# Cutting the second layer's 2304 tokens into blocks of 512, 512, 384, 320, 320 and 256 in place of four of 512 and one of 256

## Chip, cores and metric

The kernel runs on one core of one Trainium2 chip. The metric is the device time of one execution in microseconds (us); lower is better. Durations of single instructions are in nanoseconds (ns). Engines: PE is TensorE (matmuls; PEld are its weight loads), DVE is VectorE, ACT is ScalarE, POOL is GpSimd, SP is SyncE, which issues most transfers (DMA).

## What is computed

An attention over q, k, v (4 batches, 8 heads, 576 positions, 64 channels) gives a matrix of 2304 tokens by 512 channels. Two feed-forward layers follow, all in float32:

```python
x = attn_out.transpose(0, 2, 1, 3).reshape(B * S, H * D)   # 2304 x 512
h = x @ moe_w_in            # 512 -> 2048
x = np.maximum(0.01 * h, h) @ moe_w_out    # 2048 -> 512
h = x @ moe2_w_in
out = (h - np.tanh(h)) @ moe2_w_out
```

The change touches only the second layer (the last two lines).

## The kernel before

**Blocks.** Each layer goes over the tokens in blocks (PLAN, L40). The first layer has five blocks, 464 tokens and four times 460 (BLOCKS, L34). The second has four of 512 and one of 256 (BLOCKS2, L39). They run one after the other in the loop at L515. Attention work for a later block is woven into the first layer; it is not part of the second.

**One block.** The 2048 hidden units are 16 steps f of 128. In each step `gemm1` (L413) makes a 128 x n tile `hp` of hidden values, and `gemm2` (L425) adds the contribution of step f - 2 (LAG = 2) to four accumulators `acc`, each 128 x n. Operands are float32r; to keep precision each is split in a high and a low part, and a product is three matmuls: high by high, low weight by high, high weight by low. So `gemm1` has 4 chunks of channels x 3, and `gemm2` 4 output chunks x 3 matmuls for one pass over the n tokens. Every matmul loads its own 128 x 128 weights first.

**Halves.** `parts` decides how many passes: a width that is a multiple of 256 goes in pieces of 256, any other in one piece:

```python
HALF = 256
def parts(n):
    if n % HALF:
        return [slice(0, n)]
    return [slice(o, o + HALF) for o in range(0, n, HALF)]
```

A block of 512 thus takes 24 matmuls of 256 columns for each `gemm1` and each `gemm2`; one of 460 takes 12 of 460 columns; one of 256 takes 12 of 256.

**Between the two products.** In the second layer ACT takes the tanh of `hp` into `tg` (L538), DVE subtracts (`tg` = hp - tanh, L539), ACT rounds it to the high part `gh` (L541) and DVE makes the low part `gl` (L542). `hp` has two buffers, `tg` three.

**From block to block.** The next block's input `xf` comes back from DRAM (`load_x2`, L402) a whole block ahead. In the last step `convert` (L395) splits it into `xh` and `xl` (L392 on ACT, L393 on DVE). When the block's last `gemm2` is done, the four accumulators are copied to `ev` (L564 on ACT; in the very last block two of the four on DVE, L566) and sent to `out` by SP (L570). `ev` shares the three buffers of `tg`: the fourth copy needs the transfer of the first to have landed, and the next block's first two tanh need those of the second and third. The accumulators have one buffer, so the next block's first `gemm2` needs the copies done.

**Places.** `placed` (L375) gives each float32r operand tile a starting place of PLACES[idx] x 16 elements in its buffer: 80 elements in the first layer, 64 in the second. The tiles are sized for the widest block (NMAX = 512), so their strides don't depend on the block.

Of the kernel before, what the change touches and what calls it, by code (L numbers as in the profile page):

```python
# [18 lines left out]
NTOK = B * S  # L19
# [16 lines left out]
    _g = UNITS[_i:_i + BU]  # L36
    BLOCKS.append((_g[0][0] * S + _g[0][1] * QB, sum(x[2] for x in _g)))
NB = len(BLOCKS)
BLOCKS2 = [(t, min(512, NTOK - t)) for t in range(0, NTOK, 512)]  # L39
PLAN = [(0, g, n) for g, n in BLOCKS] + [(1, g, n) for g, n in BLOCKS2]  # L40
NMAX = max(n for _, _, n in PLAN)
PLACES = (5, 5, 5, 5, 5, 4, 4, 4, 4, 4)
HALF = 256
NLD = 2
U_PE = 8
# [26 lines left out]
def tile_attention_moe(  # L72
# [300 lines left out]
            wt[moe, f, half] = (hi, lo)  # L373

    def placed(tag, idx, cols, bufs=1):  # L375
        at = PLACES[idx] * 16
        t = sb.tile([128, cols + 128], F32R, tag=tag, name=tag, bufs=bufs)
        return t[:, at:at + cols]

    def new_split(idx):  # L380
        return tuple(placed(t, idx, NC * NMAX).rearrange("p (c n) -> p c n", c=NC) for t in ("xh", "xl"))
# [133 lines left out]
    for idx, (moe, g0, n) in enumerate(PLAN):  # L515
# [9 lines left out]
        for f in range(NF + LAG):  # L525
# [3 lines left out]
            if f < NF:  # L529
                hp = ps_h.tile([128, 512], F32, tag="h", name="hp")  # L530
                gemm1(moe, f, x, n, hp)
                tg = sb.tile([128, NMAX], F32, tag="tg", name="tg", bufs=3)
                gh, gl = (placed(t, idx, NMAX, 3) for t in ("gh", "gl"))
                gs[f] = (gh, gl)
                if moe == 0:
                    nc.scalar.activation(out=tg[:, :n], in_=hp[:, :n], func=ACTF.Prelu, alpha=0.01)  # L536
                else:
                    nc.scalar.activation(out=tg[:, :n], in_=hp[:, :n], func=ACTF.Tanh)  # L538
                    nc.vector.tensor_tensor(out=tg[:, :n], in0=hp[:, :n], in1=tg[:, :n], op=ALU.subtract)  # L539
                marks[:] = [  # L540
                    nc.scalar.copy(out=gh[:, :n], in_=tg[:, :n]),  # L541
                    nc.vector.tensor_tensor(  # L542
                        out=gl[:, :n], in0=tg[:, :n], in1=gh[:, :n].bitcast(F32), op=ALU.subtract
                    ),
                ]
# [94 lines left out]
```

## Time and profile before

| | us |
|---|---|
| median of 3 runs | 930.8 |
| lowest and highest of them | 928.76, 937.88 |
| the profiled execution | 930.39 |
| its span, first to last instruction | 928.6 |
| PE busy in it | 910.5 |

The profile is of one execution. Its own time lies 1.8 us above its span, and 0.4 us under the median of the runs. A row of the chain of waits gives a start, a length and a group of instructions, where each is the one that the next had to wait for. A matmul's own duration includes its way through the array, so matmuls overlap; the pace is read from the distance between starts.

### The profile page before, as it was taken

The numbers are of one execution on the slowest core, as the hardware profiler recorded it, in microseconds if no ns is written. First come the engines' busy times: TensorE is split into PE (matmuls) and PEld (weight loads), VectorE is DVE, ScalarE is ACT, GpSimd is POOL, SyncE is SP. The second block draws the span as 40 slices with busy tenths as digits, with TensorE's granted clock in tenths as the row PEclk, the third lists the DMA queues.
The fourth block names the chain that finished last, engine by engine and source line by source line (L and its number), as shares of the span: only waits on it lengthen the run. The fifth ranks groups of instructions, "written<-read, shape, count | busy, mean of one in ns | idle before, by whom it ended". The sixth has DMA issues, their size and how long they took to land.

```text
span 928.6 us, 16921 instructions
## 1 busy us (share of the span) xinstructions
PE 910.5 (98%) x7326; PEld 831.8 (90%) x7326; DVE 421.5 (45%) x747; ACT 369.0 (40%) x763; POOL 45.7 (5%) x76
## 2 busy tenths in 40 slices
PE   7989999999999999999999999999999999999997
PEld 6777788888887888888888899999999999999997
DVE  6989894444234513611376777532223223222232
ACT  2767754442244314322465655442223223322322
POOL 1011120013000100000000000000000000000000
PEclk9979999999999999999999999999999999999999
DMA  9996263137020201100466710020002000100100
GB/s 304 393 309 182 57 144 99 35 82 173 2 76 2 91 12 64 47 1 1 142 217 217 258 65 1 2 91 1 1 1 92 1 1 23 47 1 1 47 1 24
DMA packets 26186, 76.78 MB, mean 83 GB/s; under 512 B 3200, under 2 KB 7040, under 8 KB 26112
## 3 DMA queue, kind: packets, MB, share of 16 engines
q1 hardware_dynamic: 19392, 52.50, 15.9%
q0 software_dynamic: 6720, 23.21, 10.0%
q8 instruction: 57, 0.93, 0.4%
q14 instruction: 17, 0.14, 0.0%
HBM read 66.26 MB, written 9.44 MB: 82 GB/s over the span
## 4 chain that ended last, share of the span: by engine, by line
PE 91%; ACT 3%; DVE 3%; DMA 2%; issue 1%; SPq 0%; ACTq 0%
PE hp L420 42%; PE acc L432 40%; PE px L267 2%; DMA qk<-qk 1%; PE px L308 1%; ACT wm L340 1%; PE px L294 1%; PE px L209 1%; PE warm L495 1%; DVE wm L357 1%; PE px L173 1%; PE px L201 1%; DMA out<-ev 1%; ACT w L371 1%; DVE wm L350 0%
## 5 line engine op out<-in xcount | busy, mean ns | idle before, releaser
L420 PE MATMUL hp<-xh,w 128*128 128x256 f32 (+2 forms) x1792 | 395.8, 315 | 4.1 <-ACT xh L392 2.2
L432 PE MATMUL acc<-gh,w 128*128 128x256 f32 (+2 forms) x1792 | 386.7, 311 | 0.1
L420 PEld LDWEIGHTS hp<-xh,w 128*128 128x128 f32 x1792 | 292.7, 189 | 22.1 <-issue 4.1
L432 PEld LDWEIGHTS acc<-gh,w 128*128 128x128 f32 x1792 | 293.9, 188 | 13.9 <-ACT gh L541 0.3
L420 PE MATMUL hp<-xl,w 128*128 128x256 f32 (+2 forms) x896 | 281.1, 314 | 0.0
L432 PE MATMUL acc<-gl,w 128*128 128x256 f32 (+2 forms) x896 | 278.4, 311 | 0.0
L542 DVE TENSOR_TENSOR gl<-tg,gh 128x460 fp32r<-128x460 f32 (+3 forms) x160 | 101.7, 636 | 181.9 <-ACT gh L541 176.0
L420 PEld LDWEIGHTS hp<-xl,w 128*128 128x128 f32 x896 | 169.1, 189 | 6.8 <-issue 0.4
L432 PEld LDWEIGHTS acc<-gl,w 128*128 128x128 f32 x896 | 168.1, 188 | 6.8 <-DVE gl L542 0.2
L539 DVE TENSOR_TENSOR tg<-hp,tg 128x512 f32<-128x512 f32 (+1 forms) x80 | 51.0, 637 | 193.4 <-ACT tg L538 193.3
L538 ACT ACTIVATE tg<-hp 128x512 f32<-128x512 f32 (+1 forms) x80 | 44.4, 555 | 172.7 <-PE hp L420 169.2
L541 ACT CAST gh<-tg 128x460 fp32r<-128x460 f32 (+3 forms) x160 | 92.4, 577 | 49.6 <-DVE tg L539 47.9
L536 ACT ACTIVATE tg<-hp 128x460 f32<-128x460 f32 (+1 forms) x80 | 44.3, 553 | 142.6 <-PE hp L420 141.3
L372 DVE TENSOR_TENSOR w<-wm,w 128x512 fp32r<-128x512 f32 x64 | 43.0, 688 | 14.8 <-ACT w L371 13.9
L371 ACT CAST w<-wm 128x512 fp32r<-128x512 f32 x64 | 37.9, 617 | 27.8 <-DVE wm L357 22.3
L357 DVE SCALAR_TENSOR_TENSOR wm<-raw,wm 128x512 int32<-128x512 int32 x64 | 43.1, 685 | 0.7
L340 ACT ACTIVATE wm<-raw 128x512 f32<-128x512 f32 x64 | 40.9, 671 | 3.1 <-DMA raw<-wts 2.3
L564 ACT COPY ev<-acc 128x460 f32<-128x460 f32 (+3 forms) x38 | 20.1, 554 | 45.6 <-PE acc L432 32.4
L393 DVE TENSOR_TENSOR xl<-xf,xh 128x460 fp32r<-128x460 f32 (+3 forms) x40 | 24.2, 633 | 27.3 <-ACT xh L392 27.3
L392 ACT CAST xh<-xf 128x460 fp32r<-128x460 f32 (+3 forms) x40 | 21.7, 575 | 28.3 <-PE hp L420 26.8
L495 PE MATMUL warm<-band_sb,id_bf 128*128 128x192 bf16 x190 | 20.7, 265 | 3.8 <-DVE band_sb L490 3.8
L296 ACT COPY lpt<-px 128x512 f32<-128x512 f32 x16 | 9.4, 586 | 33.3 <-PE px L294 33.3
(77 smaller groups left out, 499.3 us busy)
## 6 DMA issues: line engine op xcount, KB each, us to landing
raw<-wts SPq DMA_DIRECT2D x64, 512.0 KB, 5.6
qs<-qkd POOLq DMA_DIRECT2D x12, 576.0 KB, 6.1
q<-qw POOLq DMA_DIRECT2D x16, 256.0 KB, 4.3
k<-kw POOLq DMA_DIRECT2D x16, 256.0 KB, 5.2
v<-vw POOLq DMA_DIRECT2D x16, 256.0 KB, 4.6
xf<-x2d SPq DMA_DIRECT2D x4, 1024.0 KB, 5.4
out<-ev SPq DMA_DIRECT2D x16, 256.0 KB, 3.1
x2d<-ev SPq DMA_DIRECT2D x16, 230.0 KB, 2.1
```

The lines of the kernel that those rows point to most:

```text
L340: nc.scalar.activation(out=m, in_=st[:, :, 1].bitcast(F32), func=ACTF.Abs, scale=W_SCALE)
L357: nc.vector.scalar_tensor_tensor(out=m, in0=st[:, :, 1], scalar=-0x80000000, in1=m, op0=ALU.bitwise_and, op1=ALU.bitwise_or)
L371: nc.scalar.copy(out=hi, in_=m)
L372: nc.vector.tensor_tensor(out=lo, in0=m, in1=hi.bitcast(F32), op=ALU.subtract)
L420: nc.tensor.matmul(out=hp[:, t], lhsT=w[:, cs], rhs=r[:, c, t], start=(c == 0 and i == 0), stop=(c == NC - 1 and i == 2),)
L432: nc.tensor.matmul(out=acc[m][:, t], lhsT=w[:, cs], rhs=r[:, t], start=(f == 0 and i == 0 and k == 0), stop=(f == NF - 1 and i == 2), skip ...
L495: nc.tensor.matmul(out=p[:, :3 * KB], lhsT=id_bf, rhs=band_sb.rearrange("p a w -> p (a w)"), start=True, stop=True)
L536: nc.scalar.activation(out=tg[:, :n], in_=hp[:, :n], func=ACTF.Prelu, alpha=0.01)
L538: nc.scalar.activation(out=tg[:, :n], in_=hp[:, :n], func=ACTF.Tanh)
L539: nc.vector.tensor_tensor(out=tg[:, :n], in0=hp[:, :n], in1=tg[:, :n], op=ALU.subtract)
L541: nc.scalar.copy(out=gh[:, :n], in_=tg[:, :n]),
L542: nc.vector.tensor_tensor(out=gl[:, :n], in0=tg[:, :n], in1=gh[:, :n].bitcast(F32), op=ALU.subtract),
```

## The change

The second layer's blocks become 512, 512, 384, 320, 320 and 256 tokens. 384 and 320 aren't multiples of 256, so `parts` leaves them whole: 12 matmuls of 384 or 320 columns for each `gemm1` and each `gemm2`. PLACES is now looked up by layer in place of by block, with the same values (80 elements in the first layer, 64 in the second).

```diff
-BLOCKS2 = [(t, min(512, NTOK - t)) for t in range(0, NTOK, 512)]
+SIZES2 = (512, 512, 384, 320, 320, 256)
+BLOCKS2 = [(sum(SIZES2[:i]), n) for i, n in enumerate(SIZES2)]
 PLAN = [(0, g, n) for g, n in BLOCKS] + [(1, g, n) for g, n in BLOCKS2]
 NMAX = max(n for _, _, n in PLAN)
-PLACES = (5, 5, 5, 5, 5, 4, 4, 4, 4, 4)
+PLACES = (5, 4)
...
     def placed(tag, idx, cols, bufs=1):
-        at = PLACES[idx] * 16
+        at = PLACES[PLAN[idx][0]] * 16
```

On every engine the order of the instructions is the same up to the second layer's third block; from there they follow the new widths. ACT's queue at the last joint of two blocks, before (a block of 512 ends, that of 256 begins):

```order
L392 CAST xh<-xf 128x256
L538 ACTIVATE tg<-hp 128x512
L392 CAST xh<-xf 128x256 x3
L541 CAST gh<-tg 128x512
L564 COPY ev<-acc_8018 128x512 x2
L564 COPY ev<-acc_8019 128x512 x2
L538 ACTIVATE tg<-hp 128x256 x2
L541 CAST gh<-tg 128x256 x2
L538 ACTIVATE tg<-hp 128x256
```

and after (a block of 320 ends, that of 256 begins; the source has one line more, so each line number is one higher):

```order
L393 CAST xh<-xf 128x256
L539 ACTIVATE tg<-hp 128x320
L393 CAST xh<-xf 128x256 x3
L542 CAST gh<-tg 128x320
L565 COPY ev<-acc_8172 128x320 x2
L565 COPY ev<-acc_8173 128x320 x2
L539 ACTIVATE tg<-hp 128x256 x2
L542 CAST gh<-tg 128x256 x2
L539 ACTIVATE tg<-hp 128x256
```

Nothing moved here: the queue is the same and only the ending block's tiles are narrower. SP's queue through the second layer, before (`xf` is a block's input, `out` a block's output in four transfers):

```order
L405 DMA xf<-x2d 128x4x512
L570 DMA out<-ev 128x512 x4
L405 DMA xf<-x2d 128x4x512
L570 DMA out<-ev 128x512 x4
L405 DMA xf<-x2d 128x4x256
L570 DMA out<-ev 128x512 x8
L570 DMA out<-ev 128x256 x4
```

and after:

```order
L406 DMA xf<-x2d 128x4x384
L571 DMA out<-ev 128x512 x4
L406 DMA xf<-x2d 128x4x320
L571 DMA out<-ev 128x512 x4
L406 DMA xf<-x2d 128x4x320
L571 DMA out<-ev 128x384 x4
L406 DMA xf<-x2d 128x4x256
L571 DMA out<-ev 128x320 x8
L571 DMA out<-ev 128x256 x4
```

One input transfer and four output transfers are added, and those of the later blocks are smaller; each still stands at its block's joint.

## Rows read from the trace of the kernel before

**Rows 1.** The page: busy time, and the granted TensorE clock in 40 slices.

```profile
PE 910.5 (98%) x7326; PEld 831.8 (90%) x7326; DVE 421.5 (45%) x747; ACT 369.0 (40%) x763; POOL 45.7 (5%) x76
...
PEclk9979999999999999999999999999999999999999
```

**Rows 2.** Stretches of PE: us, busy us (instructions), granted clock, DMA share, GB/s.

```profile
450.00:480.00 30.00, 30.00 (x145) 1.00 0.50 166
...
792.00:876.60 84.60, 84.60 (x749) 1.00 0.01 4
884.00:919.00 35.00, 35.00 (x300) 1.00 0.00 1
```

**Rows 3.** Chain of waits: start us, length us, group; blocks of 464, 460 and 512.

```profile
150.11 7.52 PE acc L432 x36
...
249.51 7.52 PE acc L432 x36
...
615.72 8.16 PE hp L420 x72
...
702.75 8.16 PE hp L420 x72
...
789.79 8.16 PE hp L420 x72
```

**Rows 4.** The same chain in the last block, of 256.

```profile
888.39 1.41 PE acc L432 x12
...
918.08 1.41 PE hp L420 x12
```

**Rows 5.** Timeline of PE at the second layer's start: start us, us, group, idle before.

```profile
527.10 0.28 PE L420 MATMUL hp<-xh,w 128*128 128x256 f32 x1
...
532.64 0.28 PE L420 MATMUL hp<-xl,w 128*128 128x256 f32 x1
533.83 0.51 PE L420 MATMUL hp<-xh,w 128*128 128x256 f32 x2 [0.91 <-DVE tg L539]
```

**Rows 6.** Timeline of PE: four float32 transposes, 128 columns each, in a row.

```profile
128.71 0.62 PE L294 MATMUL px<-id_sb,lpr 128*128 128x128 f32 x4
129.08 0.46 PE L420 MATMUL hp<-xh,w 128*128 128x464 f32 x1
```

**Rows 7.** Timeline of ACT and DVE at the joint of two blocks of 512.

```profile
791.25 0.59 ACT L564 COPY ev<-acc 128x512 f32<-128x512 f32 x1 [0.84 <-DMA out<-ev]
792.60 0.60 ACT L538 ACTIVATE tg<-hp 128x512 f32<-128x512 f32 x1 [0.76 <-PE hp L420]
...
793.23 0.69 DVE L539 TENSOR_TENSOR tg<-hp,tg 128x512 f32<-128x512 f32 x1 [7.32 <-ACT tg L538]
```

**Rows 8.** Timeline of all engines at the joint of 512 and 256.

```profile
876.67 0.39 PE L420 MATMUL hp<-xh,w 128*128 128x256 f32 x2
...
878.31 0.59 ACT L564 COPY ev<-acc 128x512 f32<-128x512 f32 x1 [0.85 <-DMA out<-ev]
...
879.59 0.38 ACT L538 ACTIVATE tg<-hp 128x256 f32<-128x256 f32 x1 [0.70 <-PE hp L420]
880.01 0.42 DVE L539 TENSOR_TENSOR tg<-hp,tg 128x256 f32<-128x256 f32 x1 [8.18 <-ACT tg L538]
...
880.49 0.50 PE L420 MATMUL hp<-xh,w 128*128 128x256 f32 x2 [0.93 <-DVE tg L539]
...
881.48 0.38 ACT L538 ACTIVATE tg<-hp 128x256 f32<-128x256 f32 x1 [1.50 <-DMA out<-ev]
...
882.21 0.50 PE L432 MATMUL acc<-gh,w 128*128 128x256 f32 x2
```

**Rows 9.** DMA issues: queue, count, KB each, median us to landing.

```profile
xf<-x2d SPq DMA_DIRECT2D x4, 1024.0 KB, 5.4
out<-ev SPq DMA_DIRECT2D x16, 256.0 KB, 3.1
...
out<-ev SPq DMA_DIRECT2D x4, 128.0 KB, 1.8
```

## The prediction, made before the changed kernel ran

> **What bounds the kernel now.** I read the page first: PE is busy 98% of the span and its clock is granted in full but for a slice near the start [rows 1]. Then the stretches: through the second layer PE has no idle time, at a granted clock of 1.00, the 2.4 GHz level, and with next to no DMA traffic [rows 2]. So a matmul stream sets the end, and what matters is the distance between the starts of two matmuls, the pace. The chain of waits gives it.
>
> - 512 in halves: from one block's 72 matmuls at 615.72 us to the next block's at 702.75, and again to 789.79, is 87.03 us for 768 matmuls [rows 3]: 113.3 ns for 256 columns. At 2.4 GHz 256 columns stream in 106.7 ns, so 6.6 ns come on top; I call that the excess.
> - 460 in one piece: 36 matmuls in 7.52 us [rows 3], 208.9 ns. Columns alone: 191.7. Excess 17.2 ns. The block of 464 has the same 7.52 us for 36.
> - 256, the last block: from 888.39 to 918.08 are 21 groups of 12, 252 matmuls in 29.69 us [rows 4], 117.8 ns. Excess 11.1. At the second layer's start the halves have that slower pace too: from 527.10 to 532.64 are 47 steps in 5.54 us, 117.9 ns; after the pause that ends at 533.83 the layer goes on at 113.3 [rows 5, 3]. So 256 columns have two paces, and one replaces the other at a pause of PE.
>
> That both widths of the first layer take the same time shows that the pace isn't a plain sum of columns and a constant, so 320 and 384, which no row shows, can only be bounded.
>
> **What the change does, part by part.** The same 2304 columns stream through PE in both kernels. Matmuls fall from (4 x 24 + 12) x 32 = 3456 to (2 x 24 + 4 x 12) x 32 = 3072: two blocks of 512, 2 x 768 matmuls of 256 columns, become 384 matmuls of 384 columns and 768 of 320. The price of the two old blocks is 2 x 87.03 = 174.06 us.
>
> *The new widths.* Columns alone: 384 take 160.0 ns, 320 take 133.3 ns, together 384 x 160.0 + 768 x 133.3 = 163.8 us. To that come 1152 times the excess. Bounds:
> - no excess: 163.8 us, 10.2 less than now. It can't be less, as rows 2 already show the higher clock level.
> - the 6.6 ns of the halves: 163.8 + 1152 x 6.6 = 171.4, that is 2.6 less.
> - the 17.2 ns of 460 columns: 183.7, that is 9.6 more.
> I take a straight line between the two measured widths, 6.6 ns at 256 and 17.2 at 460: 320 columns get 9.9 ns, 384 get 13.3. So 143.3 and 173.3 ns, and 384 x 173.3 + 768 x 143.3 = 66.5 + 110.1 = 176.6 us: **+2.5 us**. Why the line: 320 is nearer to 256 and 384 lies between the two, and each end of the line is a long steady row.
>
> *The joints.* Three joints of two 512s cost nothing: the block-to-block distance is the same 87.03 us as 768 matmuls at the steady pace. That of 512 and 256 costs something [rows 8]. The new block's first matmul starts at 876.67; three gemm1 of 12 matmuls at 113.3 are 4.08 us, so its first gemm2 is due at 880.75 and starts at 882.21, 1.46 us late. The cause is the three shared buffers: the fourth copy of the accumulators starts at 878.31, when the first transfer has landed; the first tanh at 879.59, which the row gives to PE, though the gemm1 it needs ended over a microsecond before: it waits for the second transfer, whose buffer it takes; DVE is then through at 880.43 and the third gemm1 can have its `hp` buffer at 880.49. At the joint of two 512s the same steps happen at nearly the same distances (fourth copy 791.25, first tanh 792.60) [rows 7], but the new block's first two gemm1 last 5.4 us and hide them. Now the joints:
> - 512 to 512, and the layer's start, stay as they are.
> - 512 to 384: two gemm1 last 24 x 173 = 4.16 us. The second transfer lands 2.92 us after the first matmul, as in rows 8; tanh and subtraction of 384 columns together lie between the 0.8 us of 256 columns (0.38 and 0.42) [rows 8] and the 1.3 of 512 (0.60 and 0.69) [rows 7], so the buffer comes free 3.7 to 4.2 us after that matmul: hidden.
> - 384 to 320, 320 to 320, 320 to 256: two gemm1 last 3.4, 3.4 and 2.7 us, but the transfers are 192 and 160 KB in place of 256; a transfer of 128 KB lands in 1.8 us where one of 256 takes 3.1 [rows 9]. Each lies between nothing and 1.46. I take 0.1 for each of the first two, near the joint that hides, and 0.6 for the last, where the pieces are shorter on both sides.
> Together 0.8 in place of 1.46: **-0.7 us**; bounds -1.5 (all hidden) and +4.4 (four joints at 1.46).
>
> *At nothing:* ACT and DVE work per column stays and both are under half busy [rows 1]; the step of a 320 block lasts 24 x 143 ns = 3.4 us, while the operations on its tile are each shorter than the 0.60 and 0.69 us of 512 columns [rows 7]. The input loads are issued a block ahead, and the shortest block lasts 45 us against 5.4 to landing [rows 9]. PLACES keeps its values. If that cover were gone it would show as PE idle inside a block, which no row of the second layer has.
>
> *The rest.* The last block keeps its 117.8 ns if PE still pauses at its start; without a pause it could go at 113.3, which is 384 x 4.5 ns = 1.7 us less. I take 0, since I expect a pause.
>
> Sum: +2.5 - 0.7 = +1.8 us on the profiled execution's 930.39: 932.2. That execution lies 0.4 under the median of the runs, so I don't correct further. About 1%, 9.3 us, is what a measurement of this kernel can tell from no change.
>
> **Rivals.**
> 1. *The halves are paced by their weight loads.* Then wider products cost nearly their columns alone. For it: the next matmul starts 0.37 us after the first of four transposes of 128 columns [rows 6], so these stand 93 ns apart, though they stream half as many columns as the halves, at 113.3. Against it: 460 columns have a larger excess, not a smaller one. Price: excess between 0 and 2.5 ns, -10.2 to -7.3, with the joints 919.5 to 922.4; 921 in the middle.
> The Trainium skill ("TensorE: Matmul & The Clock Gate", section "Back-to-back issue gap") gives N / 2.4 + 2.5 ns for a warm stream. By that rule 320 and 384 columns take 135.8 and 162.5 ns and the new blocks 166.7 us, 7.4 less than now. The trace disagrees at both widths that it has: 113.3 against 109.2 by the rule at 256, 208.9 against 194.2 at 460.
> 2. *The excess of the halves is a constant.* 6.6 ns at every width, fewer matmuls pay it less often: -2.6 - 0.7, 927.1. For it: it is the nearest row to 320. Against it: the 17.2.
> 3. *Slower: every undivided product pays the excess of 460 columns.* Place: each of the 1152 new matmuls. For it: all undivided products of the first layer, 464 and 460, pay 15.6 to 17.2 ns, and the undivided 256 of the last block pays 11.1 where halves pay 6.6. Against it: the excess of 256 columns in halves and whole differ by a pause, not by the division. Price +9.6 - 0.7: 939.3; from an excess of 8.4 ns on it is slower than before, and from 17.5 on by over 1%.
> 4. *It doesn't keep the halves' pace.* The two blocks of 512 that stay are 1536 matmuls; if the pause at 533.83 left them at 117.8 they would cost 1536 x 4.5 = 6.9 us more: 939.1. Against it: the code up to the third block is the same, and the trace shows 113.3 there for 340 us.
>
> **How the numbers follow.** The line 0.48, rival 1 0.10, rival 2 0.20, rival 3 0.15, rival 4 0.07. Faster by over 1% only by rival 1 at its far end: 0.04. Slower by over 1%: half of rival 3 and a part of rival 4, where joints come on top: 0.10. Within 1%: 0.86. The range leaves out rival 1 and the far side of rivals 3 and 4: from 926.5 (rival 2 with every joint hidden) to 939.5.
>
> **What would show it.** In the changed profile the chain should have groups of 12 in about 2.08 us in the block of 384 and 1.72 us in those of 320 (1.60 and 2.0 would be columns alone, 1.81 and 2.13 the excess of 460); the two blocks of 512 still 87.0 us each; a pause of PE of under 1 us with DVE `tg` as its releaser at the last joint, and next to none at the others. The forecast is wrong if the pace of 320 columns lies outside 140 to 151 ns, or if PE waits at joints for more than 4 us in all.

## The result and the profile after

| | before | after |
|---|---|---|
| median, us (20 runs each) | 929.73 | 938.85 |
| lowest and highest | 926.08, 947.01 | 933.0, 945.94 |
| profiled execution | 930.39 | 937.83 |
| its span | 928.6 | 936.1 |

The ratio of after to before is 1.0087, 95% interval 1.0061 to 1.0113: slower by 0.9%, about 8 us. The ratio leaves out the two executions of the kernel before that lie over 1.5% above its fastest (944.37 and 947.01 us), and it is one of means, so it isn't the quotient of the two medians. The forecast was 932.2 within 926.5 to 939.5, and no change that can be told; with 20 runs each, 0.9% can be told. The range holds the result, but near its upper end, and both terms of the sum were too low.

The chain of waits of the changed kernel (start us, length us, group), to be read against [rows 3, 4]:

```profile
532.12 4.20 PE hp L421 x24
536.32 3.15 PE acc L433 x24
...
615.63 8.16 PE hp L421 x72
...
702.67 6.24 PE hp L421 x36
...
769.23 5.50 PE hp L421 x36
774.73 1.76 PE acc L433 x12
...
820.49 5.30 PE acc L433 x36
...
825.86 3.53 DMA out<-ev
...
878.29 5.30 PE acc L433 x36
...
883.66 4.20 DMA out<-ev
...
888.85 2.93 PE hp L421 x12
891.78 1.57 PE acc L433 x12
893.35 1.36 PE hp L421 x12
...
927.35 3.41 PE acc L433 x30
```

The two blocks of 512 end at 702.67 us, where they ended before (702.75): the halves keep 113.3 ns, apart from the layer's start. Then every width shows its pace. 384 columns: 36 matmuls in 6.24 us, 173.3 ns, exactly the line's value. 320 columns: 12 in 1.76, 146.7 ns, where the line had 143.3. The block ends stand at 769.23 (384), 825.79 and 883.59 (the two of 320).

The time splits so, all from this chain and the one before:

- pace: 384 x 173.3 + 768 x 146.7 ns = 66.56 + 112.64 = 179.20 us in place of 174.06: **+5.1** (forecast +2.5);
- joints inside the new blocks: they last 883.59 - 702.67 = 180.92, so 1.72 us on top of the pace;
- the last block, to its 378th matmul (the end of the group of 30): 883.59 to 930.76 is 47.17 us; in the chain of before it was 876.83 to 923.03, 46.20. +0.97. With the line above the joints and the last block's pace give **+2.7** (forecast -0.7 and 0);
- the third block starts 0.08 earlier and the program ends 0.23 sooner behind that matmul: -0.3. (The 0.08 is what two larger differences leave, which the change has no part in: the first layer's last groups end 2.6 us earlier in this execution, and the second layer's start loses as much: PE pauses for 1.84 us where before had 0.91 [rows 5], and the groups at 532.12 and 536.32 take 4.20 and 3.15 us where 24 matmuls take 2.72, as the granted clock falls to 0.50 behind that pause.)

Together 7.5 us, the difference of the two spans.

The +2.7 hides two larger amounts. The joints inside the new blocks cost 0.24 us (384 to 320: 825.79 - 769.23 is 56.56, and 384 x 146.7 ns is 56.32) and 1.48 (320 to 320). In the last block, 378 matmuls at 113.3 ns would take 42.84 us. The changed kernel has 4.33 more, all of it from the joint and the clock behind it (below), as the steady groups stand at 1.36; the kernel before had 3.36 more, 1.46 of it from the joint [rows 8] and about 1.9 from the slower pace. So the joints cost 6.05 us in place of 1.46, which is +4.6, and the last block's pace gave back 1.9.

The two joints that cost most, in the timeline of the changed kernel (start us, us, engine line, group; in brackets the idle time before and what ended it):

```profile
827.62 0.43 ACT L565 COPY ev<-acc 128x320 f32<-128x320 f32 x1 [1.38 <-DMA out<-ev]
829.50 0.44 ACT L539 ACTIVATE tg<-hp 128x320 f32<-128x320 f32 x1 [1.45 <-DMA out<-ev]
...
830.51 0.55 PE L421 MATMUL hp<-xh,w 128*128 128x320 f32 x2 [1.23 <-DVE tg L540]
...
887.96 0.78 ACT L539 ACTIVATE tg<-hp 128x256 f32<-128x256 f32 x2 [2.43 <-DMA out<-ev]
...
888.85 0.79 PE L421 MATMUL hp<-xh,w 128*128 128x256 f32 x2 [2.45 <-DVE tg L540]
```

It is the chain of [rows 8]: the tanh waits for the second transfer to leave its buffer, DVE for the tanh, PE for DVE. It is now there at two joints, and PE's pause at the last is 2.45 us in place of 0.93. The chain above has the transfers that the two tanh waited for: 3.53 us from issue to landing at the first of the two joints, 4.20 at the second. In the kernel before the second transfer was issued at 876.67 and the tanh that waited for it started at 879.59 [rows 8], 2.9 us at most. So smaller transfers didn't land sooner. DMA issues of the changed kernel (KB each, median us to landing):

```profile
out<-ev SPq DMA_DIRECT2D x8, 256.0 KB, 2.9
...
out<-ev SPq DMA_DIRECT2D x8, 160.0 KB, 2.8
...
out<-ev SPq DMA_DIRECT2D x4, 128.0 KB, 1.7
```

The median of 160 KB is no lower than that of 256. A median mixes the four transfers of a joint, though. The first one lands at much the same time whatever its size: the fourth copy, which waits for it, starts 2.1 us after its issue at 256 KB (876.18 to 878.31 in the kernel before) and 1.9 at 160 KB (883.23 to 885.11). The second is the one that differs. The cover, two gemm1 of the next block, shrinks with the width; what it has to cover doesn't, and at these two joints it grew.

The DMA packets show what held it. At every joint of the second layer one packet of 16 KB, of the queue that carries instructions, falls among the four transfers. At the two costly joints it ran from 827.17 to 828.19 us and from 884.79 to 886.63, that is from 1.3 and 1.1 us after the issue of the second transfer; at the other joints of the two kernels it came 1.9 to 2.5 us after. At the last joint, 46 of the 48 small closing packets of the first three transfers (4 bytes, 16 for each) were done by 885.65; from then to 886.6 only the instruction packet moved, and the second transfer landed at 887.85.

The runs below have the same contrast. In 12 cases of the 13 traces the packet came within 1.5 us of the second transfer's issue, all behind blocks of 288, 320 or 384: it landed after 3.5 to 4.2 us. Where the packet came later, it landed after 1.9 to 3.2, but for two cases (4.1 in run 3, 4.9 in run 11). Run 6 has such a later packet (1.6 us) at the joint of the two 320s: its second transfer, of 160 KB too, landed after 1.95 us and PE didn't pause there. No run was made to move the packet, so this rests on what differs between the traces.

The long pause has a second price. Stretches around it (us, PE busy and count, granted clock, DMA share, GB/s):

```profile
888.00:889.00 1.00, 0.15 (x1) 0.81 0.02 8
889.00:890.00 1.00, 1.00 (x5) 0.50 0.00 0
...
892.00:893.00 1.00, 1.00 (x10) 0.98 0.00 0
```

After the pause the granted clock is 0.50, the 1.2 GHz level, for over 3 us: the group at 888.85 takes 2.93 us and that at 891.78 takes 1.57, where 1.36 is the steady length. That is 1.8 us on top of the pause itself. The length of the pause alone doesn't decide it: behind pauses of 1.88 and 2.30 us at the same joint in runs 6 and 7 below, the granted clock stays at 1.00, while behind one of 1.76 us in run 3 it falls to 0.50 too. What decides isn't shown.

### The profile page after: what moved, and what is told of

It is laid out like the page before. It is cut to its first block, busy times and chain, and to the rows that moved or that the text cites. A ratio compares the mean times of both kernels' runs of the same rounds, so it can differ in the third digit from the quotient of the medians.

```text
span 936.1 us, 16307 instructions
## 1 busy us (share of the span) xinstructions
PE 915.2 (98%) x6942; PEld 837.0 (89%) x6942; DVE 426.7 (46%) x783; ACT 375.7 (40%) x803; POOL 45.9 (5%) x76
## 4 chain that ended last, share of the span: by engine, by line
PE 87%; DMA 9%; DVE 1%; ACT 1%; issue 1%; POOL 0%; SPq 0%; ACTq 0%; POOLq 0%; DVEq 0%
PE hp L421 41%; PE acc L433 40%; DMA vs<-vd 3%; DMA qs<-qkd 2%; PE px L268 2%; DMA v<-vd 1%; PE px L309 1%; DMA out<-ev 1%; PE px L295 1%; PE px L210 1%; DMA qk<-qk 1%; PE px L174 1%; DMA x2d<-ev 1%; PE px L202 1%; DVE v L150 0%
## 5 line engine op out<-in xcount | busy, mean ns | idle before, releaser
L421 PE MATMUL hp<-xh,w 128*128 128x256 f32 (+4 forms) x1664 | 397.4, 328 | 7.8 <-DVE tg L540 5.5
L433 PE MATMUL acc<-gh,w 128*128 128x256 f32 (+4 forms) x1664 | 387.3, 323 | 0.0
L421 PE MATMUL hp<-xl,w 128*128 128x256 f32 (+4 forms) x832 | 271.5, 327 | 0.0
L433 PE MATMUL acc<-gl,w 128*128 128x256 f32 (+4 forms) x832 | 268.4, 323 | 0.0
L543 DVE TENSOR_TENSOR gl<-tg,gh 128x460 fp32r<-128x460 f32 (+5 forms) x176 | 104.3, 593 | 184.6 <-ACT gh L542 184.0
L540 DVE TENSOR_TENSOR tg<-hp,tg 128x512 f32<-128x512 f32 (+3 forms) x96 | 53.5, 558 | 195.6 <-ACT tg L539 195.6
L542 ACT CAST gh<-tg 128x460 fp32r<-128x460 f32 (+5 forms) x176 | 95.5, 542 | 53.0 <-DVE tg L540 51.2
L539 ACT ACTIVATE tg<-hp 128x512 f32<-128x512 f32 (+3 forms) x96 | 47.1, 491 | 172.6 <-PE hp L421 167.1
L394 DVE TENSOR_TENSOR xl<-xf,xh 128x460 fp32r<-128x460 f32 (+5 forms) x44 | 24.6, 590 | 26.7 <-ACT xh L393 26.7
L393 ACT CAST xh<-xf 128x460 fp32r<-128x460 f32 (+5 forms) x44 | 22.1, 540 | 27.7 <-PE hp L421 26.2
```

What stands on the lines that cost most here:

```text
L394: nc.vector.tensor_tensor(out=xl[:, c, :n], in0=src[:, c, :n], in1=xh[:, c, :n].bitcast(F32), op=ALU.subtract)
L421: nc.tensor.matmul(out=hp[:, t], lhsT=w[:, cs], rhs=r[:, c, t], start=(c == 0 and i == 0), stop=(c == NC - 1 and i == 2),)
L433: nc.tensor.matmul(out=acc[m][:, t], lhsT=w[:, cs], rhs=r[:, t], start=(f == 0 and i == 0 and k == 0), stop=(f == NF - 1 and i == 2), skip ...
L543: nc.vector.tensor_tensor(out=gl[:, :n], in0=tg[:, :n], in1=gh[:, :n].bitcast(F32), op=ALU.subtract),
```

## The experiments

The theory after the trace: A, an undivided product pays 13.3 ns on top of its columns from 288 columns or so on, twice what a half of 256 pays (6.7 ns for each started run of 256 columns), and that is about 5 us; and the joints are the other 3. Rivals: the line of the prediction for other widths, the starting place of the operands, the pace alone, the joints alone.

**1. Changed kernel, accumulator copies in buffers of their own** (two attention tiles that are dead in the second layer).

```diff
-            ev = sb.tile([128, NMAX], F32, tag="tg", name="ev", bufs=3)
+            if moe == 1:
+                ev = sb.tile([128, 512], F32, tag="lpr" if m < 2 else "lpt", name="ev", bufs=2)
+            else:
+                ev = sb.tile([128, NMAX], F32, tag="tg", name="ev", bufs=3)
```

> The changed kernel, but the copies of the second layer's accumulators go to four buffers of their own (two tiles of the attention that are dead by then) in place of the three shared with tg. Theory: of the loss, about 5 us are the pace of the new widths and about 3 us the joints, where a tanh waits for a transfer to leave its buffer; then PE has no pause at the four joints inside the layer, the profiled time falls by 3.5 to 5.5 us against the changed kernel's 937.8, and about 3 to 5 us over the kernel before are left. Rival, the pace alone: the time stays within 1.5 us of the changed kernel. Rival, the joints alone: it falls to the time of before.

Measured: 932.21 us, ratio to before 1.0013 (0.9966 to 1.0060); the profiled execution 934.37. The changed kernel had 1.0087, so the buffers take back 0.7%, some 7 us, with wide intervals. The profiled times differ by 3.5 us, the low end of what was expected, though not for the expected reason alone, as the chain shows. The gain speaks against the pace alone; the joints alone aren't excluded by these times. The chain of its profiled execution settles that, and shows something not expected:

```profile
614.98 8.48 PE hp L421 x72
...
705.43 6.29 PE hp L421 x36
...
772.50 5.28 PE hp L421 x36
...
885.14 4.09 PE hp L421 x36
```

No joint costs anything: the two blocks of 320 last 885.14 - 772.50 = 112.64 us, 768 x 146.7 ns. But from the layer's first pause on the blocks of 512 run at 8.48 / 72 = 117.8 ns, the slower pace that before had only at the layer's start and in its last block [rows 4, 5]; the 48 matmuls ahead of that pause stand 113.3 apart. And the last block is back at that faster pace, with no pause in between. That is rival 4's price, paid here by chance or by cause: runs 9 to 11 ask which.

**2. The same edit in the kernel before.**

> The kernel before with the same four buffers of their own for the copies of the second layer. Theory: its one costly joint (512 to 256) goes, and the last block stays at 113.3 ns a matmul if the slower pace of 117.8 came from the pause: 2.7 us faster (1.5 from the pause, the rest from the pace: 1.0 to 1.7). If the slower pace has nothing to do with the pause: 1.0 to 1.5 us faster. Rival, the joints cost nothing: 0.

Measured: 926.93 us, ratio 0.9943 (0.9898 to 0.9987): faster than before, though the interval all but reaches 1. Its chain has the joint of 512 and 256 without a pause, and the last block at 113.3 ns:

```profile
876.78 4.08 PE hp L420 x36
```

The profiled span is 924.9, 3.7 under before's 928.6. The joint and the slow last block were worth 3.4 of that: 378 matmuls at 113.3 are 42.84 us against the 46.20 of before. The expected 2.7 was a little low for the chain; the ratio alone would say 5 us.

**3. A sweep of widths.**

```diff
-SIZES2 = (512, 512, 384, 320, 320, 256)
+SIZES2 = (512, 448, 416, 352, 288, 288)
```

> The second layer in blocks of 512, 448, 416, 352, 288 and 288, all but the first undivided; read for the pace of each width alone. Theory A, every started run of 256 columns costs one fixed amount (6.7 ns; two runs 13.3): 200.0, 186.7, 160.0 and 133.3 ns. Theory B, the line of the prediction from 6.6 ns at 256 to 17.2 at 460: 203.3, 188.3, 158.3 and 128.3 ns. Theory C, the excess goes with where a width ends against some boundary in memory: no order in it, jumps of several ns between neighbours.

Measured: 938.93 us, one run. The steady groups of the four widths, in its chain:

```profile
613.37 7.28 PE hp L421 x36
...
691.02 6.72 PE hp L421 x36
...
770.08 1.92 PE acc L433 x12
...
832.94 1.60 PE hp L421 x12
```

448 columns take 202.2 ns, 416 take 186.7, 352 take 160.0, 288 take 133.3. The last three are theory A's to the digit and not the line's (188.3, 158.3, 128.3); the first is 2.2 ns above A, as far as 460 columns' two paces lie apart (last section); one execution doesn't tell whether 448 has a faster pace as well. So from 288 to 416 columns the excess is one constant in this execution, 13.3 ns, and at 256 it is half of that: a step, not a line. The line met 384 only because it crosses the constant there.

**4. The kernel before with 512 undivided.**

```diff
-HALF = 256
+HALF = 512
```

> The kernel before with the blocks of 512 undivided: 12 matmuls of 512 columns in place of 24 of 256. Theory A (6.7 ns for each started run of 256): 226.7 ns a matmul, 87.0 us a block, as in halves; whole kernel within 2 us of before. Theory B (the line): 19.9 ns on top, 233.2 ns, 89.6 us a block, about 10 us slower.

Measured: 936.35 us, one run; the chain:

```profile
615.20 8.40 PE hp L420 x36
```

233.3 ns: the line's value, not A's. Theory A falls at 512; the excess is 20.0 there, three times 6.7. So A holds as a table of what was measured (6.7 at 256, 13.3 from 288 to 416, 20.0 at 512) and not as a rule on started runs of 256. The time is 6.8 us above before's median on the same chip, where the line's 2.6 us for each of four blocks make 10. For the halves it says the same as the line: two products of 256 (226.7 ns) beat one of 512.

**5. The wide new blocks without the narrow ones.**

```diff
-SIZES2 = (512, 512, 384, 320, 320, 256)
+SIZES2 = (512, 512, 512, 384, 384)
```

> The second layer in blocks of 512, 512, 512, 384 and 384: one part of the change alone, the wide undivided blocks without the narrow ones. Theory (13.3 ns on top of the columns for each undivided product; joints hide where two gemm1 of the next block outlast the transfers): 384 matmuls at 173.3 ns are 66.6 us a block, two of them 133.1 against 130.6 for 512 and 256 at 113.3; no pause of over 0.5 us at a joint, as two gemm1 last 4.16 us, so the 2.7 us of the old last joint go: profiled time within 1.5 us of before. Rival, any undivided block costs a joint of over 1 us whatever its width: 3 to 5 us slower than before.

Measured: 927.19 us, one run, 1.6 under before's median of the same chip (928.78). The chain and the timeline at the joint of the two 384s:

```profile
786.11 6.24 PE hp L421 x36
...
846.42 5.21 PE acc L433 x30
```

```profile
856.52 0.49 ACT L539 ACTIVATE tg<-hp 128x384 f32<-128x384 f32 x1 [1.85 <-DMA out<-ev]
...
857.65 0.61 PE L421 MATMUL hp<-xh,w 128*128 128x384 f32 x2 [0.83 <-DVE tg L540]
```

The pace came as expected, the total just outside the 1.5 us that were. The joint of the two 384s didn't hide, where no pause of over 0.5 us was expected: PE paused for 0.83 us, since the transfer that the tanh waited for landed 3.8 us after its issue. The cover of 4.16 us wasn't quite enough. With the slower restart that joint cost 1.1 us, which is the rival's price. But it isn't paid at every undivided block, as the rival has it: the joint of 512 and 384 cost nothing, and the total has no loss of 3 to 5 us.

**6 and 7. The starting place of the operands**, in the changed kernel.

```diff
-PLACES = (5, 4)
+PLACES = (5, 5)      (run 6)
+PLACES = (5, 0)      (run 7)
```

> The changed kernel with the second layer's operands starting at 80 elements in their buffers as in the first layer, in place of 64. Theory A, the excess counts started runs of 256 columns: 320 and 384 columns stay at 146.7 and 173.3 ns, within the 1.5 ns by which a pause of PE can shift a pace. Theory C, the excess is set by where the operand starts: 320 columns move by over 3 ns.

> The changed kernel with the second layer's operands starting at 0 elements in place of 64. Theory A (started runs of 256 columns): 146.7 and 173.3 ns as before. Theory C (the starting place): 320 and 384 columns move by over 3 ns, and the halves of 256 leave 113.3 and 117.8.

Measured: 942.96 and 939.01 us, one run each. Chain of run 6, then of run 7:

```profile
700.42 8.64 PE acc L433 x72
709.06 6.25 PE hp L421 x36
...
781.00 1.76 PE acc L433 x12
```

```profile
600.73 2.83 PE acc L433 x24
...
705.32 6.29 PE hp L421 x36
772.39 5.29 PE hp L421 x36
...
891.52 1.63 PE hp L421 x12
893.15 1.36 PE acc L433 x12
```

320 columns stay at 146.7 to 146.9 ns and 384 at 173.6 to 174.7, at all three places: the place isn't the cause of their excess. The halves at 80 elements run at 120.0 ns, a pace seen nowhere else here; at 0 they show the same two as at 64, 117.8 and 113.3. So the place seems to matter for 256 columns and not for the wider ones; one execution of each doesn't say more. (The last two lines stand behind run 7's pause of 2.30 us: the granted clock didn't fall there.)

**8. The kernel before, with buffers of their own from the first layer's last block on.**

```diff
-            ev = sb.tile([128, NMAX], F32, tag="tg", name="ev", bufs=3)
+            if idx >= NB - 1:
+                ev = sb.tile([128, 512], F32, tag="lpr" if m < 2 else "lpt", name="ev", bufs=2)
+            else:
+                ev = sb.tile([128, NMAX], F32, tag="tg", name="ev", bufs=3)
```

> The kernel before (512 in halves, 256) with buffers of their own for the copies of the second layer, and of the first layer's last block too, whose joint to the second layer also shows a pause. Theory: the 5 us that the second experiment's kernel gains stay, and the pause of 1.3 us at the layer's start goes at least in part: 5 to 7 us faster than before. Rival, the layer's start waits for DVE and ACT, busy with the weights of the second layer, and not for a buffer: as the second experiment, 4 to 5 us.

Measured: 923.08 us, ratio 0.9926 (0.9902 to 0.9950): 5.7 us faster than before in the medians, faster than both kernels of this study. The timeline at the layer's start has no pause left:

```profile
531.60 0.28 PE L420 MATMUL hp<-xl,w 128*128 128x256 f32 x1
531.95 0.50 PE L420 MATMUL hp<-xh,w 128*128 128x256 f32 x2
```

Before, the same place had one of 0.91 us [rows 5]. So the layer's start did wait for a buffer, and the rival, that it waits for DVE and ACT, has no pause left to explain in this trace. But run 2's ratio lies within this one's reach; how much of the 5.7 the layer's start gives isn't told apart by the times.

**9 to 11. The kernels of runs 1 and 2 again, unedited** (the diff of run 1; run 11 has it on the kernel before), to see whether 117.8 ns belongs to a kernel or to an execution.

> The first experiment's kernel once more, unchanged, for another trace. There the two blocks of 512 ran at 117.8 ns a matmul and gave 934.4 us, while its timed runs lie around 928 and around 934. Theory: a pause of PE lets the pace of an execution fall to either 113.3 or 117.8, and that is the spread of the times: at 113.3 the two blocks of 512 take 87.0 us each and the time is near 928, at 117.8 they take 90.5 and it is near 934. Rival: the pace belongs to the kernel, its order and places; then it is 117.8 again whatever the time.

> The same kernel a third time, with the same two expectations: time near 928 with 113.3 ns, or near 934 with 117.8, if the pace is drawn at a pause; 117.8 again and no link with the time if it belongs to the kernel.

> The second experiment's kernel once more; its timed runs reach from 923 to 940. If the pace is drawn at a pause: near 923 to 927 with all second-layer matmuls at 113.3 ns, or near 938 to 940 with them at 117.8 (3456 x 4.5 ns is 15.6 us more). If the pace belongs to the kernel: 113.3 as in its first trace, whatever the time.

Measured: 927.64, 938.05 and 938.54 us. The chains of runs 9, 10 and 11:

```profile
612.20 8.16 PE hp L421 x72
...
699.24 6.24 PE hp L421 x36
...
878.43 4.09 PE hp L421 x36
```

```profile
616.24 8.48 PE hp L421 x72
...
706.70 6.36 PE hp L421 x36
...
774.54 5.28 PE hp L421 x36
...
887.18 4.24 PE hp L421 x36
```

```profile
615.70 8.48 PE hp L420 x72
```

One and the same kernel has 8.16 in one execution and 8.48 in another, and the times go with it: 927.6 against 938.1, and for the kernel of run 2, 926.6 against 938.5. The pace of the halves is a matter of the execution. Run 10 was expected near 934 and came at 938.1, since more than the two blocks of 512 (6.9 us) ran slow: 384 columns at 176.7 ns (1.3 us) and the last block at 117.8 (1.7). Run 9 is also the cleanest proof of the split: with the halves at 113.3 and no pause, its new blocks last 878.43 - 699.24 = 179.19 us, the 179.20 of the pace alone.

Run 10's chain shows who suffers. At the slower pace two blocks of 512 take 2 x 90.46 = 180.9 us (616.24 to 706.70 is one). The new blocks in the same execution take 887.18 - 706.70 = 180.5: 320 columns stay at 146.7, 384 go from 173.3 to 176.7. So the change costs 5 us of pace where the halves run fast, and in this execution none where they run slow.

## Why the prediction was right, and where it wasn't

- **The range.** It holds the result in part by luck: the forecast was +1.8 us where the spans differ by 7.5, and the upper end of 939.5 was set by rivals 3 and 4 and not by the sum. Neither of the prediction's two signs of being wrong came (320 columns at 146.7 ns lie within 140 to 151, and PE's waits at joints make 3.7 us, under 4), but the picture of the joints did not hold: a pause of 2.45 us at the last where under 1 was forecast, and one of 1.23 where next to none was.
- **What bounds the kernel.** Right. The difference of the spans is PE's pace and PE's pauses to the last 0.3 us.
- **The new widths, +2.5 us.** The direction held, the size was half. The step that failed is "320 is nearer to 256", the straight line of the excess between 6.6 ns at 256 and 17.2 at 460. Run 3 shows a step: 13.3 ns at 288, 320, 352, 384 and 416 columns. For 384 the line happened to be exact; for 320 it was 3.4 ns low, and 768 x 3.4 = 2.6 us is what the term missed. The equal times of 464 and 460 columns were quoted as a sign that the excess isn't a plain sum, and then a line was drawn all the same.
- **The joints, -0.7 us.** Wrong in sign: +4.6, beyond the bound of +4.4, and still +2.7 with what the last block's pace gave back. The step that failed is that transfers of 160 KB land sooner than those of 256, taken from the 128 KB row of [rows 9]. Their medians are 2.8 us against 2.9, and the two that PE's pauses hung on took 3.53 and 4.20, with an instruction packet among them, while the cover fell from 5.4 us to 3.5 and 2.7. The Trainium skill ("DMA: Bandwidth & Descriptors", section "Anatomy of one DMA — SWDGE (gpsimd) path") fits a transfer, on the other queue type, with about 2 us that don't depend on the size; by it 256 and 160 KB differ by an estimated 0.2 us. The first transfers of a joint agree: 2.1 us to the copy that waits at 256 KB, 1.9 at 160. The later ones don't follow the size.
- **The price of a pause.** The bound of 1.46 us for a joint was taken from a pause of 0.93. The pause of 2.45 us was followed by a granted clock of 0.50 for over 3 us, 1.8 us more, and that joint cost over 4.
- **The last block, 0.** It went at 113.3 and not 117.8 after its pause, which gave back about 1.9 us and hid that much of the joints' growth.
- **Rivals.** 1 is out: no width runs at its columns alone. 2 is out: the excess doubles above 256. 3 gives the measured time almost to the digit (939.3), for the wrong reason: the new matmuls pay 13.3 ns and not 17.2, and the joints make up the rest. 4 is real as a mechanism (runs 1, 10 and 11) but strikes the kernel before as well, so it explains the spread of the runs and not the ratio. The rule quoted under rival 1 is, in that section of the Trainium skill ("TensorE: Matmul & The Clock Gate", section "Back-to-back issue gap"), one for a single isolated matmul; a stream of weight loads and matmuls is said there to be spaced by both. So the rule's miss at 113.3 and 208.9 ns is no argument against the rival; runs 3 and 4 are.
- **Slips in the sums.** Under rival 3 the kernel gets slower than before from an excess of 9.5 ns on ((174.06 + 0.7 - 163.8) / 1152), not 8.4. Twelve matmuls of 384 columns alone take 1.92 us, not 2.0. Rival 2 with every joint hidden gives 926.3, not 926.5. And the joint of 512 and 384 was called hidden although its 4.2 us reach past the cover of 4.16; it did hide here (702.67 to 769.23 is 384 x 173.3 ns).
- **What stays open.** Why the excess of a product is 6.7, 13.3 or 20.0 ns, and what moves the pace of 256 columns between 113.3 and 117.8: it changed at pauses of PE, and in run 1 without one. Open too is why the clock fell behind some pauses and not behind others, and what, beside the instruction packet, made the two late transfers in runs 3 and 11. These were measured; nothing here shows a cause.

## What to carry to other kernels

Read the pace of a matmul as the distance of starts in a steady stretch, for the very width that is planned, before choosing block sizes: between two measured widths it can be a step. Where blocks follow each other over shared buffers, the next block's first products are the cover for the last one's transfers, and a narrower block shrinks the cover and not the wait; a separate buffer for the outgoing copy removed every such pause here and gave 0.6 to 0.7% on its own, with wide intervals. Read the landing of the very transfer that is waited for, and what else moves at that time, not the median of its row. A pause of 1.23 us cost 1.5 here; one of 2.45 us cost over 4, as the clock fell behind it.

## What the runs showed of the hardware that wasn't expected

Two executions of one kernel differ in the pace of 256-column float32r matmuls, 113.3 or 117.8 ns, for the whole second layer (3456 of them in run 11: 15.6 us), at a granted clock of 1.00 in either. The first layer's 460-column matmuls have two paces too, 208.9 ns in the kernel before's profile [rows 3] and 206.7 in run 2's, whose chain reads:

```profile
440.26 7.44 PE acc L432 x36
```

The two go together: where the first layer's last block ran at 208.9 ns (before, the changed kernel, runs 3, 10 and 11) the second layer began at 117.8, and where it ran at 206.7 with operands at 64 or 0 elements (runs 1, 2, 5, 7, 8 and 9) it began at 113.3. So the slower pace is there before the second layer starts. 320-column matmuls had one pace, 146.7 ns, in every execution.
